# An attention block's per-unit output copy, split between VectorE and ScalarE

## The chip, the cores and the metric

The kernel runs on one core of a Trainium2 chip. The metric is the device time of one execution in microseconds (us); the figure compared is the median over several runs. A profile is one execution recorded by the hardware, with every instruction's start and length on each engine: TensorE (PE, with its weight loads apart as PEld), VectorE (DVE), ScalarE (ACT), GpSimd (POOL) and SyncE (SP), which here issues most of the transfers.

## The reference

A gated attention block over 2048 tokens of width 512, with 32 heads of width 16 and a feed-forward width of 1376:

```python
xn = layernorm(x)
q, k, v = split_heads(xn @ wqkv)                 # 32 heads of 16
s = softmax(q k^T / 4) v, heads joined, @ wo     # attention
g = silu(gelu(xn @ w1 + b1) @ w2 + b2)           # gate
out = x + s * g
```

## The kernel before, in words

A first stage (to about 480 us) normalises x, makes q, k, v and the feed-forward part, and writes the gate's input to memory. The change lies in the second, the attention stage.

The 32 heads form 8 groups of 4, and the 2048 queries 4 chunks of 512. A *unit* u is one chunk of one group: 32 units. A unit goes through the 2048 keys in 16 *steps* of 128 keys. What a step n does is written out as a string of letters (`ORDER`, the loop from L963): in nearly all of the stage `TXSTTSTYV`, in its last 21 steps `TTTTV`.

- `T` (`t_one`, L729): a score matmul (L736) for one head, 128 keys by 512 queries, into one of four PSUM buffers used in turn (`pst`, three of them, and `ps`), and behind it on ScalarE its exponential (L738) into SBUF. Four a step, one for each head.
- `S`, `X`, `Y` (`s_op`, L209): score matmuls of another layout for units still to come (L183), of which VectorE takes row maxima (L189, three reduces a step). They use three more PSUM buffers in turn. `X` and `Y` are two halves of one such matmul; a GpSimd token lies between them.
- `V` (`pv_step`, L795): the product of the step before: four matmuls (L801), one for each head, which add 128 keys' exponentials times v into a PSUM buffer `pv` of 128 rows by 512 queries. Each matmul stands as two instructions in the profile, so a V product is eight records. There is one such buffer (the pool `ps_v`); a unit's first V product starts a new sum in it.

Behind a unit's last V product (`k == NT - 1`, L804), its sums are copied from `pv` to an SBUF tile `os` of 128 by 512: for all but the last unit one ScalarE instruction (L808), and for the last two instructions of 256 columns (`HC`), one on ScalarE (L810) and one on VectorE (L811). In the step after, `o_move` (L818) has SyncE move the rows of `os` (a transfer of the denominators, L821, and four of the heads' outputs, L824); `o_den` (L827) takes reciprocals eight steps later, and `o_div` (L836) divides after that. `o_move`, `o_den`, `o_div` and the loads of later units are hung on step and place by `at` (L916), and run behind the `T` of that place.

Every engine takes its instructions in the order in which the loop gives them, each engine for itself; between engines, semaphores hold an instruction until its inputs are there and its output buffer is free.

Of the kernel before, what the change touches and what calls it, by code (L numbers as in the profile page):

```python
# [10 lines left out]
AF = mybir.ActivationFunctionType  # L11
# [29 lines left out]
HC = CH // 2  # L41
# [7 lines left out]
def fused(ctx: ExitStack, tc: tile.TileContext, x, wqk, wv, wo, w1, b1, w2, b2, out):  # L49
    nc = tc.nc  # L50
# [75 lines left out]
    def slot(i, shape, dtype=F32):  # L126
        return big.tile(list(shape), dtype, name=f"slot{i}")
# [33 lines left out]
    def tick():  # L161
        for e in later:
            e[0] -= 1

    def flush():
        while later and later[0][0] <= 0:
            u = later.pop(0)[1]
            run_off()
            s_end1(u)
            s_end2(u)  # L170
# [38 lines left out]
    def s_op(op):  # L209
        if op == "S":  # L210
            if whole:
                s_whole(whole.pop(), 1)
            else:
                whole.append(jobs.pop(0))
                s_whole(whole[0], 0)
        elif op == "X":
            if not cut:
                cut[:] = [jobs.pop(0), 0]
            ps, pool = s_tile(True)
            x = s_mm(ps, cut[0], 0, 0, cut[1] * HC, HC)  # L220
            token = nc.gpsimd.nop().ins
            tc.add_manual_dep(token, x.name, SYNC, reason="row tile done")
            cut[2:] = [ps, pool, token]
            run_off()
        else:
            job, n, ps, pool, token = cut
            y = s_mm(ps, job, 1, HC, n * HC, HC)
            tc.add_manual_dep(y, token.name, SYNC, reason="other row tile")
            s_max(ps, job, slice(0, 2), n)
            s_ring.append(pool)  # L230
            cut[1] += 1
            if n:
                cut.clear()
# [487 lines left out]
    def t_tile():  # L721
        turns[0] += 1
        if turns[0] < 5:
            pool = (ps_m, ps_x, ps_a, ps_b)[turns[0] - 1]
        else:
            pool = ps_m if turns[0] % 4 == 1 else ps_t
        return pool.tile([P, CH], F32, name="pst" if pool is ps_t else "ps")

    def t_one(u, k, p, a):  # L729
        g = u // NCH  # L730
        if (u, k) not in PT:
            PT[u, k] = slot(3 + len(PN) % 3, (P, GH, CH))
            PN.append(1)
        ps = t_tile()
        r = slice(64 * a, 64 * a + 3 * DH + 2)
        nc.tensor.matmul(ps, kts[g % KB][p][r, k * P:(k + 1) * P],  # L736
                         QT[u][r, p, :], start=True, stop=True)
        nc.scalar.activation(PT[u, k][:, 2 * p + a, :], ps, AF.Exp, scale=SCALE)  # L738
# [53 lines left out]
        nc.gpsimd.tensor_sub(wo_l[:, k], WR.pop(k), wo_h[:, k].bitcast(F32))  # L792

    PV, OS, DN, DR = {}, {}, {}, {}
    def pv_step(u, k):  # L795
        g = u // NCH
        if k == 0:
            PV[u] = ps_v.tile([P, CH], F32, name="pv")
        for j in range(GH):
            h = (g * GH + j) * VW  # L800
            nc.tensor.matmul(PV[u][32 * j:32 * j + 32, :], vsb[:, k, h:h + 32], PT[u, k][:, j, :],  # L801
                             start=(k == 0), stop=(k == NT - 1))
        del PT[u, k]
        if k == NT - 1:  # L804
            OS[u] = wb.tile([P, CH], F32, name="os", bufs=1)
            pv = PV.pop(u)
            if u < NU - 1:
                nc.scalar.activation(OS[u], pv, AF.Copy)  # L808
            else:
                nc.scalar.activation(OS[u][:, :HC], pv[:, :HC], AF.Copy)  # L810
                nc.vector.tensor_copy(OS[u][:, HC:], pv[:, HC:])  # L811
# [110 lines left out]
    def due(n):  # L922
        return min(4 * L, 4 * LEAD + max(0, 3 * n - 1))
# [39 lines left out]
    for n in range(L + 1):  # L963
        ua, ka = divmod(n, 16)
        want = due(n) - due(n - 1)
        i = 0
        for op in ORDER[want] if n > 1 else ("TTTTV", "TTSTSVT")[n]:
            if op in "SXY":
                s_op(op)
            elif op == "V":  # L970
                if n:
                    pv_step(*divmod(n - 1, 16))
                for _ in range(4):
                    tick()
                flush()
            else:
                if EARLY <= 4 * n + i < 4 * L:
                    t_one(ua, ka, i % 2, 1 - i // 2)
                for f, args in todo.get((n, i), []):
                    f(*args)  # L980
                i += 1
# [52 lines left out]
```

## Time and profile before

| | us |
|---|---|
| median of 3 runs (1598.42 to 1599.15) | 1598.57 |
| profiled execution | 1600.85 |
| its span, first to last instruction | 1598.8 |
| TensorE busy | 1589.6 (99%) |
| VectorE busy | 1383.4 (87%) |
| ScalarE busy | 1260.6 (79%) |
| GpSimd busy | 374.8 (23%) |
| granted TensorE clock, share of full | 0.998 |

TensorE's matmuls overlap each other, and their ends are modelled, so 99% doesn't say that TensorE is at its peak. What a stage waits for is read from the waits and from the order of starts in the timeline. Rows of the timeline give the start, the length, the engine, the line, the operation with output and inputs, the shape, the count, and in brackets the idle time before it with what ended it. Rows of groups give the count, then the busy time and the mean length of one in ns, then the idle time ahead of them. Rows of waits give who waited for whom: the sum, the count and the longest.

### The profile page before, as it was taken

The numbers are of one execution on the slowest core, as the hardware profiler recorded it, in microseconds if no ns is written. First come the engines' busy times: TensorE is split into PE (matmuls) and PEld (weight loads), VectorE is DVE, ScalarE is ACT, GpSimd is POOL, SyncE is SP. The second block draws the span as 40 slices with busy tenths as digits, with TensorE's granted clock in tenths as the row PEclk, the third lists the DMA queues.
The fourth block names the chain that finished last, engine by engine and source line by source line (L and its number), as shares of the span: only waits on it lengthen the run. The fifth ranks groups of instructions, "written<-read, shape, count | busy, mean of one in ns | idle before, by whom it ended". The sixth has DMA issues, their size and how long they took to land.

```text
span 1598.8 us, 32213 instructions
## 1 busy us (share of the span) xinstructions
PE 1589.6 (99%) x12132; PEld 915.7 (57%) x12132; DVE 1383.4 (87%) x2259; ACT 1260.6 (79%) x2520; POOL 374.8 (23%) x396
## 2 busy tenths in 40 slices
PE   9999999999999999999999999999999999999998
PEld 7899999999994444444444444444444444444445
DVE  7499898989888999999999999999999999999734
ACT  4333433434349999999999999999999999999984
POOL 4135575756640001000100200100010000000143
PEclk9999999999999999999999999999999999999999
DMA  6625342454332113111410311311131111110252
GB/s 205 149 58 147 121 136 97 151 143 133 113 97 60 37 31 69 29 38 44 79 32 24 70 41 30 59 41 28 28 74 27 32 29 37 34 29 22 59 195 96
DMA packets 74651, 116.89 MB, mean 73 GB/s; under 512 B 23012, under 2 KB 24292, under 8 KB 73320
## 3 DMA queue, kind: packets, MB, share of 16 engines
q1 hardware_dynamic: 71036, 102.41, 23.1%
q0 software_dynamic: 3264, 12.35, 3.9%
q8 instruction: 96, 1.57, 0.4%
q14 instruction: 59, 0.48, 0.1%
q10 hardware_dynamic: 196, 0.07, 0.0%
HBM read 84.35 MB, written 25.97 MB: 69 GB/s over the span
## 4 chain that ended last, share of the span: by engine, by line
PE 96%; issue 2%; POOL 1%; DVE 1%; DMA 0%; ACT 0%; POOLq 0%; SPq 0%; DVEq 0%
PE pv L801 31%; PE ps L183 18%; PE pst L736 15%; PE ps L587 12%; PE pst L587 7%; PE ps L736 5%; PE pv L587 2%; PE ps L80 2%; PE ps L459 1%; POOL ol L874 0%; PE pst L459 0%; PE pst L80 0%; POOL gx L907 0%; PE pst L441 0%; DMA xt<-in_x 0%
## 5 line engine op out<-in xcount | busy, mean ns | idle before, releaser
L189 DVE TENSOR_REDUCE mx<-ps 128x2 f32<-128x512 f32 x2048 | 1299.9, 685 | 149.6 <-PE ps L183 85.0
L738 ACT ACTIVATE slot<-pst 128x512 f32<-128x512 f32 x1533 | 833.8, 612 | 21.6 <-PE ps L736 8.9
L801 PE MATMUL pv<-slot,vsb 128*32 128x512 f32 x4096 | 545.2, 605 | 0.0
L183 PE MATMUL ps<-kt,slot 48*128 48x512 f32 (+1 forms) x1364 | 393.6, 376 | 0.0
L736 PE MATMUL pst<-qt,kt 50*128 50x512 f32 x1149 | 372.7, 430 | 0.6 <-DVE gt L669 0.4
L736 PEld LDWEIGHTS pst<-qt,kt 50*128 50x128 f32 x1149 | 178.9, 184 | 280.2 <-ACT slot L738 264.3
L738 ACT ACTIVATE slot<-ps 128x512 f32<-128x512 f32 x515 | 315.3, 613 | 3.8 <-PE ps L736 0.7
L183 PEld LDWEIGHTS ps<-kt,slot 48*128 48x128 f32 x1364 | 210.6, 184 | 34.8 <-DVE mx L189 21.0
L587 PE MATMUL ps<-slot,w1h 64*128 64x512 f32 x1088 | 218.6, 393 | 0.0
L183 PE MATMUL ps<-kt,qz 48*128 48x512 f32 x512 | 213.9, 418 | 0.0
L183 PE MATMUL ps<-slot,slot 48*128 48x512 f32 (+1 forms) x598 | 172.8, 376 | 0.0
L736 PE MATMUL ps<-qt,kt 50*128 50x512 f32 x387 | 162.5, 422 | 0.0
L587 PEld LDWEIGHTS ps<-slot,w1h 64*128 64x128 f32 x1088 | 152.8, 185 | 6.6 <-ACT junk L601 0.8
L801 PEld LDWEIGHTS pv<-slot,vsb 128*32 128x32 f32 x4096 | 80.6, 108 | 120.2 <-issue 112.3
L587 PE MATMUL ps<-slot,w1l 64*128 64x512 f32 x544 | 142.2, 392 | 0.0
L378 POOL TENSOR_TENSOR hl<-hg,hh 128x512 fp32r<-128x512 f32 x76 | 96.8, 1295 | 127.5 <-ACT hh L377 85.6
L601 ACT ACTIVATE junk<-ident_r 1x1 f32<-1x1 f32 x92 | 18.0, 196 | 123.4 <-PE pst L587 114.0
L736 PE MATMUL pst<-qt,slot 50*128 50x512 f32 x384 | 112.5, 415 | 0.0
L251 POOL CAST nmh<-nm 128x16 fp32r<-128x16 f32 x32 | 6.3, 196 | 415.0 <-PE ps L183 174.4
L183 PEld LDWEIGHTS ps<-kt,qz 48*128 48x128 f32 x512 | 93.7, 183 | 16.8 <-DVE mx L189 0.3
L183 PEld LDWEIGHTS ps<-slot,slot 48*128 48x128 f32 x598 | 92.6, 184 | 15.6 <-DVE mx L189 11.1
L736 PEld LDWEIGHTS ps<-qt,kt 50*128 50x128 f32 x387 | 71.0, 184 | 44.0 <-ACT slot L738 42.8
(159 smaller groups left out, 1703.6 us busy)
## 6 DMA issues: line engine op xcount, KB each, us to landing
raw<-in_w SPq DMA_DIRECT2D x88, 256.0 KB
qk_h<-hh SPq DMA_DIRECT2D x32, 256.0 KB
qk_l<-hl SPq DMA_DIRECT2D x32, 256.0 KB
qt<-qk_h SPq DMA_DIRECT2D x128, 64.0 KB
slot<-qk_h SPq DMA_DIRECT2D x92, 64.0 KB
xt<-in_x SPq DMA_DIRECT2D x16, 256.0 KB
g_d<-gt POOLq DMA_DIRECT2D x16, 256.0 KB, 3.6
qt<-qk_l SPq DMA_DIRECT2D x64, 64.0 KB
```

The lines of the kernel that those rows point to most:

```text
L80: nc.tensor.matmul(ps, lhs[a], rhs[b], start=first and n == 0, stop=last and n == 2)
L183: return nc.tensor.matmul(ps[:, c0:c0 + w], QS[u][r, p, qi * P:(qi + 1) * P], kts[u // NCH % KB][p][r, k0:k0 + w], start=True, stop=True).ins
L189: nc.vector.tensor_reduce(MX[u][:, 2 * p:2 * p + 2, qi, ki][:, heads, parts], ps.rearrange("p (n c) -> p n c", c=HC), axis=AX.X, op=OP.max)
L251: nc.gpsimd.tensor_copy(hl[:, 0], nm)
L378: nc.gpsimd.tensor_sub(hl, raw, hh.bitcast(F32))
L459: nc.tensor.matmul(pq["q", g, c], W1[g][i][:, k * P:(k + 1) * P], (xh, xl)[j][c][:, k], start=n == 0 and k == 0, stop=n == 2 and k == KT - 1)
L587: i = nc.tensor.matmul(ps, lhs[r], rhs[r], start=first, stop=last).ins
L601: i = nc.scalar.activation(junk[:, :1], ident_r[:1, :1].bitcast(F32), AF.Copy).ins
L736: nc.tensor.matmul(ps, kts[g % KB][p][r, k * P:(k + 1) * P], QT[u][r, p, :], start=True, stop=True)
L738: nc.scalar.activation(PT[u, k][:, 2 * p + a, :], ps, AF.Exp, scale=SCALE)
L801: nc.tensor.matmul(PV[u][32 * j:32 * j + 32, :], vsb[:, k, h:h + 32], PT[u, k][:, j, :], start=(k == 0), stop=(k == NT - 1))
```

## The change

The copy of a unit's sums, for all units but the last, becomes two instructions of 256 columns each. VectorE's, for the upper columns, is given where the whole copy was, behind the unit's last V product. ScalarE's, for the lower columns, is put on a list and given in the next step, behind that step's first `T` (that is, behind its first exponential on ScalarE) and ahead of what is hung on that place, `o_move` among it. The last unit's copy stays.

```diff
     PV, OS, DN, DR = {}, {}, {}, {}
+    halves = []
+
+    def os_half():
+        if halves:
+            o, pv = halves.pop()
+            nc.scalar.activation(o[:, :HC], pv[:, :HC], AF.Copy)
+
     def pv_step(u, k):
...
             OS[u] = wb.tile([P, CH], F32, name="os", bufs=1)
             pv = PV.pop(u)
             if u < NU - 1:
-                nc.scalar.activation(OS[u], pv, AF.Copy)
+                nc.vector.tensor_copy(OS[u][:, HC:], pv[:, HC:])
+                halves.append((OS[u], pv))
             else:
                 nc.scalar.activation(OS[u][:, :HC], pv[:, :HC], AF.Copy)
                 nc.vector.tensor_copy(OS[u][:, HC:], pv[:, HC:])
...
                 if EARLY <= 4 * n + i < 4 * L:
                     t_one(ua, ka, i % 2, 1 - i // 2)
+                os_half()
                 for f, args in todo.get((n, i), []):
                     f(*args)
                 i += 1
```

## The prediction

> **What bounds the kernel now.** First the page, for the span, the chain that ended last and the costliest groups.
>
> ```profile
> span 1598.8 us, 32213 instructions
> ...
> PE 96%; issue 2%; POOL 1%; DVE 1%; DMA 0%; ACT 0%; POOLq 0%; SPq 0%; DVEq 0%
> ...
> L189 DVE TENSOR_REDUCE mx<-ps 128x2 f32<-128x512 f32 x2048 | 1299.9, 685 | 149.6 <-PE ps L183 85.0
> L738 ACT ACTIVATE slot<-pst 128x512 f32<-128x512 f32 x1533 | 833.8, 612 | 21.6 <-PE ps L736 8.9
> L801 PE MATMUL pv<-slot,vsb 128*32 128x512 f32 x4096 | 545.2, 605 | 0.0
> ```
>
> The chain is TensorE's, so what counts is the time from one V product (L801) to the next, a step. Then the waits: weight loads of TensorE wait for an exponential, for a row maximum, and 30 times for the copy that the diff touches.
>
> ```profile
> PEld pst L736 <- ACT slot L738: 306.9, 401, 0.8
> ...
> PEld ps L183 <- DVE mx L189: 32.4, 186, 0.3
> ...
> PEld pv L801 <- ACT os L808: 7.0, 30, 0.3
> ```
>
> What a wait costs is read from the timeline. Here is TensorE around one unit end (columns: start, length, engine, line). The V product at 579.66 is the last of its unit.
>
> ```profile
> 579.66 1.06 PE L801 MATMUL pv<-slot,vsb 128*32 128x512 f32 x8
> 580.66 0.50 PE L736 MATMUL pst<-qt,kt 50*128 50x512 f32 x1
> ...
> 581.78 1.07 PE L801 MATMUL pv<-slot,vsb 128*32 128x512 f32 x8
> ...
> 584.17 1.07 PE L801 MATMUL pv<-slot,vsb 128*32 128x512 f32 x8
> 585.17 0.50 PE L736 MATMUL pst<-qt,kt 50*128 50x512 f32 x1
> ...
> 585.74 0.40 PE L183 MATMUL ps<-slot,slot 48*128 48x512 f32 x1
> 585.86 0.39 PE L736 MATMUL ps<-qt,kt 50*128 50x512 f32 x1
> ...
> 586.18 1.06 PE L801 MATMUL pv<-slot,vsb 128*32 128x512 f32 x8
> ...
> 588.31 0.64 PE L801 MATMUL pv<-slot,vsb 128*32 128x512 f32 x4
> ```
>
> Steps: 2.12, 2.39, 2.01, 2.13 us. Ordinary steps alternate between 2.01 and 2.13; the one after the unit's copy takes 2.39. The reader is to see that the first score matmul of a step (580.66, 585.17) starts 1.00 behind the V product: nothing moves before the V product is through. ScalarE over the same time:
>
> ```profile
> 580.62 0.62 ACT L738 ACTIVATE slot<-ps 128x512 f32<-128x512 f32 x1
> 581.10 0.63 ACT L808 ACTIVATE os<-pv 128x512 f32<-128x512 f32 x1
> 581.58 1.62 ACT L738 ACTIVATE slot<-pst 128x512 f32<-128x512 f32 x3
> 583.01 0.68 ACT L738 ACTIVATE slot<-ps 128x512 f32<-128x512 f32 x1
> ...
> 584.92 0.73 ACT L738 ACTIVATE slot<-ps 128x512 f32<-128x512 f32 x1
> 585.70 1.57 ACT L738 ACTIVATE slot<-pst 128x512 f32<-128x512 f32 x3
> 587.15 0.62 ACT L738 ACTIVATE slot<-ps 128x512 f32<-128x512 f32 x1
> ```
>
> Back to back, ScalarE starts one instruction every 0.48 (580.62, 581.10, 581.58), so four exponentials are 1.92, under the ordinary step. The copy makes five, 2.40: that is the 2.39 step. In it TensorE waits where it does not in other steps, at the fourth score matmul. In the 2.13 steps it waits for VectorE instead:
>
> ```profile
> 583.74 0.18 PEld L736 LDWEIGHTS ps<-qt,kt 50*128 50x128 f32 x1 [0.30 <-ACT slot L738]
> ...
> 587.76 0.18 PEld L183 LDWEIGHTS ps<-slot,slot 48*128 48x128 f32 x1 [0.17 <-DVE mx L189]
> ```
>
> Against an ordinary mean of 2.07, the copy thus costs 2.39 - 2.07 = 0.32 at a unit end. There are 31 such copies, 30 of them in this stage: about 9.6 us is all that can be won.
>
> The second kind of unit end has the V product of 2.01 ahead of the long step:
>
> ```profile
> 780.82 1.06 PE L801 MATMUL pv<-slot,vsb 128*32 128x512 f32 x8
> ...
> 782.83 1.06 PE L801 MATMUL pv<-slot,vsb 128*32 128x512 f32 x8
> ...
> 785.20 1.06 PE L801 MATMUL pv<-slot,vsb 128*32 128x512 f32 x8
> ...
> 787.21 0.64 PE L801 MATMUL pv<-slot,vsb 128*32 128x512 f32 x4
> ```
>
> The two steps from the unit's last V product on are 579.66 to 584.17 = 4.51 in the first kind and 780.82 to 785.20 = 4.38 in the second.
>
> **The change part by part.** The copy's own rows, and the one place where it is already halved, the last unit:
>
> ```profile
> L808 ACT ACTIVATE os<-pv x31: 621/628/629, 513.8 to 1527.5; 128x512 f32<-128x512 f32 x31
> ...
> L810 ACT ACTIVATE os<-pv x1: 386/386/386, 1576.9 to 1576.9; 128x256 f32<-128x256 f32 x1
> L811 DVE COPY os<-pv x1: 425/425/425, 1577.3 to 1577.3; 128x256 f32<-128x256 f32 x1
> ```
> ```profile
> 1576.88 0.39 ACT L810 ACTIVATE os<-pv 128x256 f32<-128x256 f32 x1 [1.14 <-PE pv L801]
> ...
> 1577.30 0.42 DVE L811 COPY os<-pv 128x256 f32<-128x256 f32 x1 [1.61 <-ACT os L810]
> ```
>
> Removed: 31 ScalarE copies, 0.48 of the engine each. Added on ScalarE: 31 halves of 0.39, behind the first exponential. An exponential lasts 0.60 and keeps the engine 0.48, so 0.12 overlaps; the half keeps it 0.39 - 0.12 = 0.27 (bounds: 0.27, and the whole copy's 0.48). The Trainium skill (ScalarE: Activation LUTs, What ACT_TABLE_LOAD costs) gives 186 + 0.833 N ns for an activation with immediate operands, 93 of it overlapped; as an estimate 0.40 for the half and 0.31 of the engine. For 512 columns it would give a spacing of 0.52, where the trace has 0.48; the rows decide, and by the page the sum below would be 0.3 us more over 30 units.
>
> Added on VectorE: 31 halves of 0.42, 0.34 of the engine (a reduce of 0.68 comes every 0.60, so 0.08 overlaps). VectorE's rows:
>
> ```profile
> 579.29 1.89 DVE L189 TENSOR_REDUCE mx<-ps 128x2 f32<-128x512 f32 x3 [0.23 <-PE ps L183]
> ```
> ```profile
> 583.44 1.89 DVE L189 TENSOR_REDUCE mx<-ps 128x2 f32<-128x512 f32 x3 [0.24 <-PE ps L183]
> 585.82 1.89 DVE L189 TENSOR_REDUCE mx<-ps 128x2 f32<-128x512 f32 x3 [0.50 <-PE ps L183]
> ```
>
> Its three reduces of the step end at 581.18, so the half starts about 581.10 (1.44 behind the V product, which has ended by then) and ends 1.87 behind it. It fills the idle time ahead of the next reduce (0.24 to 0.50) and pushes that by 0.1 to 0.34. Cost taken: nothing; the cover is the idle time just named, and the 0.3 by which the next V product will be late (next paragraph). Without it the waits of L183 for L189 grow: up to 0.11 a unit, the gap between the two ordinary steps.
>
> The moved half decides. The next V product starts a new sum in the same PSUM buffer (one buffer, L798), so it needs both halves done. Now it starts 0.05 behind the whole copy (581.10 + 0.63 = 581.73, then 581.78), which is when TensorE gets there anyway. With the change, from the unit's last V product: 1.00 to the first score matmul; 0.53 more until a free ScalarE starts on it (585.17 to 585.70); 0.48 until the half starts; 0.39 for the half; 0.05 to the V product. Sum 2.45, in place of 2.12 and 2.01. It doesn't depend on what ScalarE did before, since the exponential can't start earlier. So the step in front of the long one grows by 0.33 to 0.44.
>
> The long step behind it goes: the exponentials after the half start 2.28, 2.76 and 3.24 behind the V product, the last ends at about 3.9, and the fourth score matmul would come 0.69 behind the first (585.17 to 585.86), at 2.45 + 1.00 + 0.69 = 4.14. So no wait for ScalarE; VectorE's last reduce (third from 1.78 at 0.60 each, ended by 3.7) is through as well. What is late next is nothing: I take the fast 2.01. The two steps are then 2.45 + 2.01 = 4.46, against 4.51 and 4.38: -0.05 and +0.08.
>
> One term is left: the alternation. A 2.01 step is followed by a 2.13 one, and the change shifts which comes first; in the first kind this may take back up to 0.11. So the first kind is -0.05 to +0.06, the second +0.08. At equal weight (both kinds recur; a choice) that is +0.04 a unit, x30 = +1.3 us; both ends together -0.05 and +0.11, so -1.5 to +3.3 us. For the half's length the dear end is the whole copy's 0.63, +0.24 a unit, +7 us; I take 0.39, the row of the same shape.
>
> The 31st unit end lies in the output stage, where only exponentials and output products run; there the copy isn't what a step waits for, and I take zero, between -0.3 and +0.3. SP's five loads of the copy (the move) are asked for 0.35 later; they are used 8 steps later, some 16 us, so nothing. No DMA, matmul or exponential is added or removed.
>
> **Sum.** The profiled execution took 1600.85 us, 2.28 above the median of 1598.57; with +1.3 it would be 1602.2, and the median 1599.9. About 0.2% (3.2 us) is what a measurement of this kernel can tell from no change, so this is no change.
>
> **Rivals.** *Faster: the next V product isn't held.* Then the step ahead stays, and the long one falls to four exponentials and a half, 4 x 0.48 + 0.27 = 2.19, in place of 2.39: 0.20 x 30 = 6.0 us less, 1592.6. For it speaks that the engine time of the copy is what fills the 2.39 step. It decides if the half ends within 2.07 of the last V product; the 1.00 and the 0.53 ahead of its exponential speak against.
>
> *Slower: the late V product isn't made good.* The step behind it is 2.13 or 2.19, because the displaced reduces, or the exponentials behind the half, hold a score matmul after all. Then 4.58 to 4.64 against a mean of 4.45: +0.13 to +0.19, x30 = +3.9 to +5.7 us, 1602.5 to 1604.3. It decides when the last reduce ends later than the score matmul that needs its buffer (585.17 to 585.74, so 2.45 + 1.00 + 0.57 = 4.02 behind the unit's last V product), or the last exponential later than 4.14; I have 3.7 and 3.9, so the margin is two to three tenths.
>
> *Much slower: the halves in a chain.* The row at 1577.30 shows that VectorE's half waited 0.03 past the end of ScalarE's, though they share no column. So after the change ScalarE's half waits for VectorE's. If one more reduce stood ahead of that, it would end at 1.87 + 0.60 = 2.47, the V product would come at 2.47 + 0.03 + 0.39 + 0.05 = 2.94, another 0.49 a unit: +14.7 us, 1614.6. It decides where VectorE's half ends later than 2.01. Against it: the copy is issued right behind the step's last reduce, ending at 1.87. The Trainium skill (PSUM — Partial Sum Buffer, PSUM bank collisions raise a hardware error) says that two engines may not be in one bank and quadrant at once, disjoint columns included; by that rule the wait is there, and the trace agrees.
>
> **Chances.** The forecast 0.58, faster 0.10, not made good 0.27, chain 0.03, anything else 0.02. The forecast's own range is 1597.1 to 1601.9; its upper end and the second rival give slower by over 0.2% 0.33, no change 0.56, faster 0.11. The range of 8 in 10 runs from 1597.0 to 1604.5: it leaves out the faster rival, the chain and a tail.
>
> **What would show it.** The V product behind a unit end 2.45 behind the last one, its weights waiting for ScalarE's half (0.3 to 0.4, 30 times; now 7.0 us in all); the following step 2.01, with no wait of the fourth score matmul; VectorE's copy between two reduces, 1.3 to 1.5 behind the V product. I am wrong if that wait is short (faster), or if the following step still takes 2.13 or more (slower).

## The result and the profile after

The changed kernel takes 1602.49 us (median of 12 runs, 1601.83 to 1602.92) against 1598.33 us (12 runs), a ratio of 1.0024 with a 95% interval of 1.0016 to 1.0032: 4.2 us slower. That is inside the range of 8 in 10 (1597.0 to 1604.5), but above the forecast's own, which ended at 1601.9, and past the 3.2 us that the prediction took as the bound for "no change". The profiled execution took 1602.27 us with a span of 1600.5.

Single executions with a granted clock of 0.998 or lower took 1.5 to 5 us longer than the others of the same kernel; the profile before is one of them, and so are six of the 17 of the changed kernel with the row maxima shifted (below), whose two medians are 1601.75 and 1601.73 without them. The two profiles differ by less than 4.2, since the first stage of the one before is 2.3 us longer (its first V product starts at 480.85, that of the one after at 478.50; neither kernel differs there). The attention stage alone, from the start of the first V product to the start of the last, shows the change: 1094.92 before, 1098.94 after, +4.02. Where a kernel was profiled twice, the stage repeated to within 0.15.

First the page's busy row and the waits of the changed kernel (sum, count, longest). The copy's lines are now L815 (VectorE) and L800 (ScalarE), the V product's is L808.

```profile
PE 1584.1 (99%) x12132; PEld 917.4 (57%) x12132; DVE 1386.4 (87%) x2290; ACT 1255.9 (78%) x2520; POOL 376.8 (24%) x396
```
```profile
PEld ps L183 <- DVE mx L189: 39.5, 219, 0.3
...
PEld pv L808 <- ACT os L800: 17.9, 30, 0.7
...
PE pv L808 <- ACT os L800: 8.4, 30, 0.4
```

The V product's wait for the copy went from 7.0 to 17.9 in its weight loads, and for 8.4, 0.28 each time, the matmuls themselves now sit idle for it, which the waits before didn't have at all. Then the timeline of the unit end that the prediction shows: TensorE (start, length), ScalarE, VectorE.

```profile
577.61 1.06 PE L808 MATMUL pv<-slot,vsb 128*32 128x512 f32 x8
578.60 0.50 PE L736 MATMUL pst<-qt,kt 50*128 50x512 f32 x1
...
580.06 1.06 PE L808 MATMUL pv<-slot,vsb 128*32 128x512 f32 x8 [0.27 <-ACT os L800]
581.06 0.50 PE L736 MATMUL pst<-qt,kt 50*128 50x512 f32 x1
...
582.08 0.64 PE L808 MATMUL pv<-slot,vsb 128*32 128x512 f32 x4
```
```profile
579.14 0.60 ACT L738 ACTIVATE slot<-pst 128x512 f32<-128x512 f32 x1
579.63 0.38 ACT L800 ACTIVATE os<-pv 128x256 f32<-128x256 f32 x1
579.89 1.10 ACT L738 ACTIVATE slot<-pst 128x512 f32<-128x512 f32 x2
```
```profile
577.24 1.89 DVE L189 TENSOR_REDUCE mx<-ps 128x2 f32<-128x512 f32 x3 [0.24 <-PE ps L183]
579.04 0.42 DVE L815 COPY os<-pv 128x256 f32<-128x256 f32 x1
579.38 1.88 DVE L189 TENSOR_REDUCE mx<-ps 128x2 f32<-128x512 f32 x3
581.71 0.69 DVE L189 TENSOR_REDUCE mx<-ps 128x2 f32<-128x512 f32 x1 [0.46 <-PE ps L183]
```

The chain of starts can be read off: V product 577.61, first score matmul 578.60, its exponential 579.14, the half 579.63 to 580.01, the next V product 580.06. That is 2.45. The step behind is 580.06 to 582.08, 2.02. VectorE's copy comes right behind the step's third reduce. It pushes the next one from 1.65 to 1.77 behind the V product (581.31 behind 579.66 before, 579.38 behind 577.61 here), and that run of reduces still ends long before the one after begins (0.46 of idle time).

So the two steps behind a unit's last V product take 4.47, where 4.46 was forecast. Before, they took 4.50 on average in the first kind and 4.42 in the second (units 1 to 28, 14 of each), so these pairs make -0.04 and +0.05, in all 0.2 of the 4.0. The rest lies in the steps between, and shows only over whole units, from a unit's first V product to the next unit's. Worked out from the starts (us; of these, 2 and 6 are of the first kind):

```
unit   before   after
7      33.38    33.44    nothing else in the unit
2      33.56    33.65    one small reduce (L248) within it
6      33.77    33.84    one small reduce, and what follows from it
8      33.36    33.64    its small reduce lay in the long step
24     33.36    33.61    the same
```

Seven units, each fourth from 4 to 28, pay 0.25 to 0.29 (1.92 together). The 22 others pay 0.04 to 0.11 (median 0.07), but for unit 13 with 0.36; the 22 make 1.85, and the stage's two ends 0.24. The seven have their excess in the second step. Before the change, TensorE and VectorE:

```profile
749.47 1.07 PE L801 MATMUL pv<-slot,vsb 128*32 128x512 f32 x8
...
751.85 1.07 PE L801 MATMUL pv<-slot,vsb 128*32 128x512 f32 x8
...
753.86 0.64 PE L801 MATMUL pv<-slot,vsb 128*32 128x512 f32 x4
```
```profile
751.11 0.69 DVE L189 TENSOR_REDUCE mx<-ps 128x2 f32<-128x512 f32 x1 [0.16 <-PE ps L183]
751.72 0.27 DVE L248 TENSOR_REDUCE nm<-mx 128x16 f32<-128x128 f32 x1
```

And after the change, with a weight load's wait:

```profile
750.28 1.07 PE L808 MATMUL pv<-slot,vsb 128*32 128x512 f32 x8
...
752.59 0.64 PE L808 MATMUL pv<-slot,vsb 128*32 128x512 f32 x4
```
```profile
750.52 0.28 DVE L248 TENSOR_REDUCE nm<-mx 128x16 f32<-128x128 f32 x1
750.71 2.56 DVE L189 TENSOR_REDUCE mx<-ps 128x2 f32<-128x512 f32 x4
```
```profile
752.05 0.18 PEld L183 LDWEIGHTS ps<-kt,slot 48*128 48x128 f32 x1 [0.30 <-DVE mx L189]
```

When a unit of row maxima is complete, a small reduce (L248, 0.28) is put between VectorE's three, and delays the next ones. Wherever it falls into an ordinary step, that step is 2.2 to 2.3 long, in both kernels. There are 22 of them in units 1 to 29, three in every four units, and one in three began in the long step behind the copy (749.47 to 751.85, 2.38, no longer than the others of its kind). That step waited for ScalarE and had room on VectorE. The change removed the long step, and the small reduce then stood in a step without room: 750.28 to 752.59, 2.31.

### The profile page after: what moved, and what is told of

Its sections match the earlier page's. It is cut to its first block, busy times and chain, and to the rows that moved or that the text cites. A ratio compares the mean times of both kernels' runs of the same rounds, so it can differ in the third digit from the quotient of the medians.

```text
span 1600.5 us, 32358 instructions
## 1 busy us (share of the span) xinstructions
PE 1584.1 (99%) x12132; PEld 917.4 (57%) x12132; DVE 1386.4 (87%) x2290; ACT 1255.9 (78%) x2520; POOL 376.8 (24%) x396
## 4 chain that ended last, share of the span: by engine, by line
PE 90%; ACT 5%; issue 2%; DVE 1%; POOL 1%; DMA 0%; POOLq 0%; ACTq 0%; SPq 0%; DVEq 0%
PE pv L808 30%; PE ps L183 17%; PE pst L736 14%; PE ps L587 12%; PE pst L587 7%; PE ps L736 5%; ACT slot L738 4%; PE pv L587 2%; PE ps L80 2%; PE ps L459 1%; ACT os L800 1%; POOL ol L882 0%; POOL gx L915 0%; PE pst L80 0%; DMA xt<-in_x 0%
## 5 line engine op out<-in xcount | busy, mean ns | idle before, releaser
L189 DVE TENSOR_REDUCE mx<-ps 128x2 f32<-128x512 f32 x2048 | 1299.3, 685 | 146.4 <-PE ps L183 89.6
L808 PE MATMUL pv<-slot,vsb 128*32 128x512 f32 x4096 | 545.3, 605 | 8.4 <-ACT os L800 8.4
L183 PE MATMUL ps<-kt,slot 48*128 48x512 f32 (+1 forms) x1364 | 390.8, 376 | 0.1
L738 ACT ACTIVATE slot<-ps 128x512 f32<-128x512 f32 x515 | 311.3, 605 | 5.7 <-PE ps L736 3.0
L183 PEld LDWEIGHTS ps<-kt,slot 48*128 48x128 f32 x1364 | 211.0, 184 | 38.9 <-DVE mx L189 27.1
L183 PE MATMUL ps<-kt,qz 48*128 48x512 f32 x512 | 213.5, 417 | 0.0
L183 PE MATMUL ps<-slot,slot 48*128 48x512 f32 (+1 forms) x598 | 171.2, 375 | 0.0
L808 PEld LDWEIGHTS pv<-slot,vsb 128*32 128x32 f32 x4096 | 80.6, 108 | 129.3 <-issue 110.5
L183 PEld LDWEIGHTS ps<-kt,qz 48*128 48x128 f32 x512 | 93.7, 183 | 17.1 <-DVE mx L189 0.3
L183 PEld LDWEIGHTS ps<-slot,slot 48*128 48x128 f32 x598 | 92.8, 184 | 16.6 <-DVE mx L189 12.2
```

What stands on the lines that cost most here:

```text
L183: return nc.tensor.matmul(ps[:, c0:c0 + w], QS[u][r, p, qi * P:(qi + 1) * P], kts[u // NCH % KB][p][r, k0:k0 + w], start=True, stop=True).ins
L189: nc.vector.tensor_reduce(MX[u][:, 2 * p:2 * p + 2, qi, ki][:, heads, parts], ps.rearrange("p (n c) -> p n c", c=HC), axis=AX.X, op=OP.max)
```

## The experiments

The theory (A in the expectations): the time is an account of the unit end, in which the V product's longer wait for ScalarE's half and the shorter step behind nearly cancel, with VectorE's half free; what is left over is the small reduce that lost its cover. The rivals: VectorE's half, which displaces three reduces, is the cost (B); only the moment at which ScalarE's half ends counts (C). Times are medians; the kernel before, on the same chips, took 1598.35 to 1598.70.

**ScalarE's half left out.**

```diff
             o, pv = halves.pop()
-            nc.scalar.activation(o[:, :HC], pv[:, :HC], AF.Copy)
...
+                nc.gpsimd.memset(OS[u][:, :HC], 1.0)
                 nc.vector.tensor_copy(OS[u][:, HC:], pv[:, HC:])
```

> Leaves out ScalarE's half: the lower 256 columns of each unit's sums but the last are filled with ones by GpSimd, so the output is not the reference's; VectorE's half stays where it is. Theory A (the time is the account of the unit end: the V product waits about 0.4 us more for ScalarE's half, the step behind it regains most of that; VectorE's half is free): both go, the two steps behind a unit's last V product fall from 4.47 to about 4.14, 30 x 0.33 = 10 us below the changed kernel, about 1592. Rival B (VectorE's half, which displaces three row maxima, is what costs): VectorE's part is unchanged, the wait of the row maxima stays, and the time stays at 1600 or above.

Measured: 1591.92, a ratio to before of 0.9959 (0.9944 to 0.9974), 10.6 below the changed kernel. Its unit end:

```profile
577.56 1.06 PE L808 MATMUL pv<-slot,vsb 128*32 128x512 f32 x8
...
579.69 1.06 PE L808 MATMUL pv<-slot,vsb 128*32 128x512 f32 x8
...
581.81 0.64 PE L808 MATMUL pv<-slot,vsb 128*32 128x512 f32 x4
```

The steps are 2.13 and 2.12, ordinary ones, although VectorE's half is there: units with nothing else in them take 33.09 to 33.15, which is 16 steps of the ordinary mean, 2.07. B falls: its wait (L183 for L189) is 42.5 here, more than the 39.5 of the changed kernel, in a kernel that is 10 us faster. So ScalarE's half is worth 10 us in the changed kernel. Against the kernel before, leaving it out wins 6.7 (6.4 of them in the stage), not the prediction's "about 9.6 us is all that can be won": that counted 0.32 a unit end, where whole units are 0.26 shorter than before, and the seven whose small reduce lost its cover only 0.07.

**ScalarE's half ahead of the first exponential.**

```diff
             else:
+                os_half()
                 if EARLY <= 4 * n + i < 4 * L:
                     t_one(ua, ka, i % 2, 1 - i // 2)
-                os_half()
```

> ScalarE's half is given ahead of the next step's first exponential instead of behind it. Theory A with the halves in a chain: ScalarE's half can't start before VectorE's ends, 1.87 behind the V product (first kind) or 1.76 (second), ends at 2.26 or 2.15, the next V product comes at 2.31 or 2.20 in place of 2.455; but ScalarE idles from 1.44 on, its fourth exponential ends at 4.1 to 4.2, and the fourth score matmul of the next step waits, so that the step behind is 2.3 to 2.4: the two steps 4.6 to 4.7, +0.15 to +0.2 a unit, 1607 to 1609. Rival C (the only thing that counts is how early ScalarE's half ends): 0.14 to 0.25 a unit less, 1595 to 1598.

Measured: 1604.84, 1.0039 (1.0024 to 1.0054). C falls: the half ends earlier, and the kernel is slower by 2.4 than the changed one. But the loss is only about half of the least that theory A gave (1607). The rows of TensorE, ScalarE and a wait:

```profile
578.18 1.06 PE L808 MATMUL pv<-slot,vsb 128*32 128x512 f32 x8
...
580.51 1.07 PE L808 MATMUL pv<-slot,vsb 128*32 128x512 f32 x8
...
582.89 0.64 PE L808 MATMUL pv<-slot,vsb 128*32 128x512 f32 x4
```
```profile
580.07 0.38 ACT L800 ACTIVATE os<-pv 128x256 f32<-128x256 f32 x1 [0.30 <-DVE os L815]
```
```profile
ACT os L800 <- DVE os L815: 9.8, 31, 0.6
```

The two steps are 2.33 and 2.38, 4.71, at the upper end of what was expected. ScalarE waits 31 times, 0.3 each, for VectorE's half, which shares no column with its own: the halves do run in a chain, and for who waits for both, splitting shortens nothing. The buffer is free 2.27 behind the V product (at 580.45); with the whole copy of the kernel before it was 2.07. Whether the wait comes from the buffer `pv` that both halves read or from the tile `os` that both write, no run separates. Part of the missing loss is the small reduce once more: here the step behind is long again (2.38, with ScalarE late), and the reduce at every fourth unit end is hidden in it again (2.38 to 2.39 with it, the same without). Those seven units are 0.07 shorter than in the changed kernel, the others 0.13 longer, which makes 1.4 us; the rest of the miss isn't worked out.

**The whole copy, behind the first exponential.**

```diff
-            nc.scalar.activation(o[:, :HC], pv[:, :HC], AF.Copy)
+            nc.scalar.activation(o, pv, AF.Copy)
...
-                nc.vector.tensor_copy(OS[u][:, HC:], pv[:, HC:])
                 halves.append((OS[u], pv))
```

> The whole copy on ScalarE, as before the change, but behind the next step's first exponential; nothing on VectorE. Theory A: the V product comes 1.00 + 0.53 + 0.49 + 0.63 + 0.05 = 2.70 behind the last one, the step behind it is 2.01: 4.71 against 4.47, +0.24 a unit, +7.3 us over the changed kernel, about 1609.8. Rival B: without VectorE's half it is no slower than the changed kernel, 1600 to 1602.5.

Measured: 1608.61, 1.0064 (1.0047 to 1.0080), 6.1 above the changed kernel where 7.3 was expected.

```profile
578.16 1.06 PE L808 MATMUL pv<-slot,vsb 128*32 128x512 f32 x8
...
580.83 1.07 PE L808 MATMUL pv<-slot,vsb 128*32 128x512 f32 x8 [0.47 <-ACT os L800]
...
582.83 0.64 PE L808 MATMUL pv<-slot,vsb 128*32 128x512 f32 x4
```

The copy lasts 0.59 here, not 0.63 (580.18 to 580.77), so the V product comes 2.67 behind the last. VectorE has no half at all, and the kernel is the slowest: B once more falls. The place behind the exponential costs 10 us against the same copy right behind the V product.

**A quarter on ScalarE, three on VectorE.**

```diff
-            nc.scalar.activation(o[:, :HC], pv[:, :HC], AF.Copy)
+            nc.scalar.activation(o[:, :QC], pv[:, :QC], AF.Copy)
...
-                nc.vector.tensor_copy(OS[u][:, HC:], pv[:, HC:])
+                nc.vector.tensor_copy(OS[u][:, QC:], pv[:, QC:])
```

`QC` is 128 columns.

> ScalarE copies 128 columns, VectorE 384, at the same places. Theory A: ScalarE's part lasts 0.28 in place of 0.39, so the V product comes 2.35 behind the last one in place of 2.455; VectorE's part ends at 1.99, still ahead of ScalarE's start at 2.02; the step behind stays 2.01. 0.1 x 30 = 3.2 us less than the changed kernel, about 1599.3. Rival B (VectorE's part costs): slower than the changed kernel, 1604 or more.

Measured: 1599.24, 1.0004 (0.9995 to 1.0012); the changed kernel on the same chip 1601.94, 1.0022 (1.0013 to 1.0031), 3.2 above the kernel before and not the 4.2 that was expected; its stage repeats (1098.80).

> The changed kernel once more, beside the next three on the same chip: 1602.5, 4.2 us above the kernel before.

```profile
577.59 1.06 PE L809 MATMUL pv<-slot,vsb 128*32 128x512 f32 x8
...
579.95 1.07 PE L809 MATMUL pv<-slot,vsb 128*32 128x512 f32 x8 [0.16 <-ACT os L801]
...
581.98 0.64 PE L809 MATMUL pv<-slot,vsb 128*32 128x512 f32 x4
```

2.36 and 2.03: the wait follows ScalarE's columns one to one, 0.11 less for 128 columns less (0.38 to 0.27), while VectorE's part grows to 0.55 and the step behind stays at 2.00 to 2.04. The kernel is back at the time before the change, not under it.

**All of it on VectorE.**

```diff
-                nc.scalar.activation(OS[u], pv, AF.Copy)
+                nc.vector.tensor_copy(OS[u], pv)
```

> The whole copy on VectorE, behind the V product; ScalarE does nothing. Theory A: the copy takes VectorE 0.60 from 1.44 (first kind) or 1.33 (second) on, the V product comes at 2.17 or 2.07; three reduces then run from 2.04 to 3.92, later than the score matmul that needs the buffer (about 3.74), so that the step behind is 2.3: two steps 4.4 to 4.5, 1598 to 1602. If VectorE's time were free at any length: 4.13, 1590. Rival B (VectorE's time is the cost, at the rate of the half): twice the changed kernel's loss, 1606.

Measured: 1599.03, 1.0002 (0.9992 to 1.0011). The rows of TensorE and of its weight loads:

```profile
577.70 1.07 PE L801 MATMUL pv<-slot,vsb 128*32 128x512 f32 x8
...
579.86 1.07 PE L801 MATMUL pv<-slot,vsb 128*32 128x512 f32 x8
...
582.20 0.64 PE L801 MATMUL pv<-slot,vsb 128*32 128x512 f32 x4
```
```profile
581.66 0.18 PEld L183 LDWEIGHTS ps<-slot,slot 48*128 48x128 f32 x1 [0.30 <-DVE mx L189]
```

2.16 and 2.34. The V product comes hardly later than an ordinary one, but the step behind is nearly as long as with ScalarE's copy, now held by VectorE. So with no part on ScalarE, half the copy leaves the step behind an ordinary one and the whole doesn't. The three quarters were free under the cover of the V product's wait for ScalarE; how much VectorE could take without that, no run shows.

**The row maxima's work one reduce earlier**, in the changed kernel, so that the small reduce of each fourth unit end falls into the step in which the V product waits.

```diff
-        return min(4 * L, 4 * LEAD + max(0, 3 * n - 1))
+        return min(4 * L, 4 * LEAD + 3 * n)
...
-ORDER = {0: "TTTTV", 3: "TXSTTSTYV"}
+ORDER = {0: "TTTTV", 2: "TTSTSTV", 3: "TXSTTSTYV"}
...
-        for op in ORDER[want] if n > 1 else ("TTTTV", "TTSTSVT")[n]:
+        for op in ORDER[want] if n > 1 else ("TTTTV", "TTXSTSYVT")[n]:
```

> The changed kernel with the row maxima's work one reduce earlier, so that the reduce which ends a unit of maxima (the small one over 128 columns, 0.28) falls into the step in which the V product waits for ScalarE's half, at the seven unit ends where it now falls into the step behind. Theory A: those seven steps fall from 2.31 to about 2.12 with no change elsewhere, 7 x 0.2 = 1.4 us less than the changed kernel, 1601.1. If the small reduce isn't what makes these steps long: 1602.5.

Measured: 1601.97, 1.0027 (1.0017 to 1.0038): no gain that the median shows. The stage did get shorter, 1097.63 against 1098.80 and 1098.94. Unit by unit, the seven are 0.13 to 0.21 shorter, and the others the same to 0.04. TensorE and VectorE at the seventh unit's end:

```profile
749.07 1.07 PE L808 MATMUL pv<-slot,vsb 128*32 128x512 f32 x8 [0.27 <-ACT os L800]
...
751.09 1.07 PE L808 MATMUL pv<-slot,vsb 128*32 128x512 f32 x8
...
753.22 0.64 PE L808 MATMUL pv<-slot,vsb 128*32 128x512 f32 x4
```
```profile
748.05 0.41 DVE L815 COPY os<-pv 128x256 f32<-128x256 f32 x1
748.39 0.68 DVE L189 TENSOR_REDUCE mx<-ps 128x2 f32<-128x512 f32 x1
748.98 0.28 DVE L248 TENSOR_REDUCE nm<-mx 128x16 f32<-128x128 f32 x1
```

The small reduce now begins in front of the V product of 749.07, and the step that was 2.31 is 2.13. Where the gain went is asked by the same kernel again, and by the same shift on the kernel before, where the small reduce had cover all along.

> The changed kernel with the row maxima's work one reduce earlier, once more, since its first median (1601.97, between 1601.41 and 1606.64) showed nothing of the 1.2 us that its attention stage is shorter. Theory A: stage again 1.2 us shorter than the changed kernel's 1098.9; the total 1601 if the rest is as in the other kernels, 1602 if the earlier work costs elsewhere.

> Control: the kernel before, with the row maxima's work one reduce earlier. The small reduce of the seven unit ends stays within or right at the long step, in which VectorE has time. Theory A: no change of the attention stage, 1598.3 to 1598.9. If the earlier work itself costs something elsewhere (first or last stage), it shows here: the kernel with the earlier work and the change had a stage of attention 1.2 us shorter than the changed kernel, and yet the same total; then about 1599.5.

Measured on one chip: 1602.12, 1.0027 (1.0017 to 1.0036), and 1599.28, 1.0007 (0.9998 to 1.0016), beside 1598.35. The stage is 1097.72, and 1095.04 for the shifted kernel before. With the shift in both, the change costs 2.7 in the stage (1097.72 - 1095.04), without it 4.0. So the small reduce at the seven unit ends is 1.3 of the 4.0.

The shift itself costs some 0.9 outside the stage (1599.28 against 1598.35, though its interval reaches 1). Most of that lies just ahead of the stage. TensorE in the kernel before, from the last product of the first stage in this buffer to the first V product, and then the same with the shift:

```profile
477.99 0.39 PE L587 MATMUL pv<-w2h,hl 64*128 64x512 f32 x1
...
480.85 1.07 PE L801 MATMUL pv<-slot,vsb 128*32 128x512 f32 x8
```
```profile
475.56 0.39 PE L587 MATMUL pv<-w2h,hl 64*128 64x512 f32 x1
...
478.88 0.38 PE L183 MATMUL ps<-slot,slot 48*128 48x256 f32 x1 [0.39 <-POOLq L221]
479.19 1.06 PE L801 MATMUL pv<-slot,vsb 128*32 128x512 f32 x8
```

That is 2.86 and 3.63; in the profiles of all kernels with the shift it is 3.62 to 3.63, in those of all others 2.85 to 2.86. The pair `X`, `Y` that the last line of the diff puts ahead of the first V product waits there for its GpSimd token. These 0.8 take most of what the seven unit ends gain.

**Quarter and shift together.** Both of the diffs above.

> Both of the two changes: ScalarE 128 columns and the row maxima's work one reduce earlier. Theory A: 3.2 + 1.4 = 4.6 us below the changed kernel, 1597.9, just below the kernel before. Where the shorter hold no longer covers the small reduce: 1599.3, as with the quarter alone.

Measured: 1599.98, 1.0008 (0.9999 to 1.0017), not below the quarter alone. The V product then comes 2.35 behind the last, and the small reduce falls behind it, into a step that takes 2.2 at all seven ends: the shorter wait no longer covers it, the second of the two cases expected. The stage is 1095.46, 0.5 above that of the kernel before. No version that computes the reference's output beat the kernel before.

## Why the prediction was right, and where it was off

- *What bounds.* The step from V product to V product, with ScalarE late at unit ends: right. Without ScalarE's half the stage is 10.4 us shorter than in the changed kernel.
- *The moved half decides.* The sum of 1.00, 0.53, 0.48, 0.39 and 0.05 gave 2.45; measured 2.45 to 2.46 at the 29 unit ends behind the first (2.52 there). The quarter (2.34 to 2.36) and the whole copy (2.66 to 2.67) follow the same sum with their own lengths to 0.02, so the mechanism is shown, not argued. The prediction's aside on the Trainium skill (ScalarE: Activation LUTs, What ACT_TABLE_LOAD costs), 0.3 us more over 30 units, counts the half alone; with the 0.52 that it works out for an exponential, as an estimate by that page, another 0.04 x 30 = 1.2 us would come on top.
- *The step behind* at the fast 2.01: measured 2.00 to 2.02 at all 30. The rival "not made good" therefore did not happen, although the time came out at its price (1602.5). That the range had room for the measured time is owed to that price: luck, as far as the number goes.
- *VectorE's half at nothing:* right. With it and without ScalarE's, a unit end is an ordinary one. Its cover was read one and two steps too late, though: at its own place the idle time was 0.13 (581.18 to 581.31), not 0.24 to 0.50, and the next reduce moved by 0.12.
- *The chain of halves:* there, and not binding in the changed kernel, since ScalarE's half starts 2.02 behind the V product and VectorE's ends at 1.85. With ScalarE's half ahead of the exponential it binds, by 0.3 each time. That agrees with the rule that the prediction cites from the Trainium skill (PSUM — Partial Sum Buffer, PSUM bank collisions raise a hardware error), that two engines may not be in one bank and quadrant at once, but the two halves also share the tile `os`.
- *Mis-sized: the alternation*, "the first kind is -0.05 to +0.06". The prediction put the 2.12 ahead of the long step in the first kind down to the unit end, as something the change takes away. Measured over whole units, units 2 and 6 (first kind) pay 0.09 and 0.07, as much as unit 7 of the second (0.06). In the first kind the alternation takes back its whole 0.11, more than the pair of steps gave, where the prediction counted half of it. With the median of 0.07 a unit that is 30 x 0.07 = 2.1 us, against the 1.3 that was forecast.
- *Missing: the small reduce.* The sum named no work that the long step itself covered. Seven small reduces (L248) lay in it, and lost their cover with it: 1.3 us. The prediction had asked of each added edit what hides it, but not of the step that went away what it had hidden.

Together 2.1 + 1.3 = 3.4 of the stage's 4.0. Another 0.3 is one step of unit 13 (918.74 to 921.14, 2.41); ahead of it the exponential of a first score matmul begins 0.36 late (918.60, 0.89 instead of 0.53 behind the 917.71 of its matmul). The step of unit 13 is 2.38 to 2.42 in every profile with parts on both engines and ScalarE's behind the exponential, and 2.13 or less with VectorE's half alone or ScalarE's whole copy alone; why is open. The rest, 0.3, is the two ends of the stage and rounding.

## What to carry to other kernels

A long step is also a shelter: before removing it, look for what the other engines do in it that would be late elsewhere. An instruction that frees a buffer is priced by when it ends, counted from the product that it follows, and moving it behind an instruction with its own input to wait for puts that wait into the chain; here 0.38 of copying was held back by 1.00 of matmul, 0.53 of latency and 0.48 of exponential. And a copy split over two engines from one PSUM buffer doesn't halve the time until the buffer is free, when the halves go one behind the other.

## What the runs showed of the hardware that was not expected

- A reduce on VectorE that is about 0.02 too late goes with 0.11 more of step. Ordinary steps alternate between 2.01 and 2.12; in every second one a weight load of L183 waits for VectorE (the rows at 587.76), and its matmul starts 0.59 instead of 0.57 behind the step's first. That the 0.11 comes from weights no longer loaded ahead is a guess that no run tests. The alternation goes on for whole units; a small reduce shifts its phase and costs 0.2 in either, 2.20 in place of 2.01 or 2.31 in place of 2.12.
- ScalarE's copy lasted 0.59 behind one exponential and 0.63 in the middle of a run of them, with the same shape; the half 0.38, the quarter 0.27.
- VectorE's copies from PSUM took 0.42, 0.55 and 0.68 for 256, 384 and 512 columns: 0.13 for each further 128.
